# Windowed attention and a two-layer MLP on one core: another first load, another mask tile and another order of work for batch 0

## The chip, the core and the metric

The kernel runs on one core of a Trainium2 chip. The core has a matrix engine (TensorE, PE in the profile; its weight loads are listed as PEld), a vector engine (DVE), a scalar engine (ACT), GpSimd (POOL) and a queue engine (SP). POOL and SP issue the DMAs of this kernel. The metric is the device time of one execution in microseconds (us); lower is better. Three executions of the kernel before took 336.78, 336.99 and 338.26 us.

## The reference

Inputs are q, k and v of shape 8 batches x 8 heads x 576 positions x 64, and two weight matrices, 512 x 2048 and 2048 x 512, all in float32.

```python
scores = scale * np.matmul(q, k.transpose(0, 1, 3, 2))
rel = pos[:, None] - pos[None, :]
mask_plain = (rel >= 0) & (rel < window)                                # window 32
mask_dil = (rel >= 0) & (rel < window * dilation) & (rel % dilation == 0)  # dilation 4
masks = np.stack([mask_plain if h < H // 2 else mask_dil for h in range(H)], axis=0)
...                                   # softmax over the masked scores, attn @ v
x = attn_out.transpose(0, 2, 1, 3).reshape(B * S, H * D)                # 4608 x 512
h = x @ w_in
g = h * (1.0 / (1.0 + np.exp(-h)))
return (g @ w_out).astype(np.float32)
```

The first four heads look at the last 32 positions; the other four look at 32 positions that are 4 apart. Within one class of positions modulo 4 the second kind is the first kind again, on 144 positions.

## The kernel before, in words

**Two kinds of heads.** In the code z is the kind: z=0 the plain heads, z=1 the dilated ones, whose positions are sorted into four classes. Queries are taken 32 at a time against 64 keys. A score tile holds four such blocks in its 128 rows, and blocks of 64 columns side by side; one block of columns is called a slot.

**One batch of attention** goes through these helpers. `load_qk` and `load_v` issue the DMAs on POOL, which turn float32 into float16 on the way. `transpose` turns q and k on TensorE (16-bit transposes into PSUM) and copies them out on DVE and ACT. `scores` multiplies q and k (`score`, `score_class`, and `last_scores` for the 64 last positions), and adds mask and scale on DVE (L459, L468); L475 takes maxima. `exps` runs on ACT, either slot by slot with sums (L507), or in one instruction after `shift` has subtracted the maxima on DVE. `normal` divides on DVE (L516 to L523), `turn` and `turned` transpose the probabilities and copy them (L532, L540), `values` and `last_values` multiply with v (L565, L628), and `finish` casts the result into xT (L641). v lies in the tile vw; `shift_v` (`shift_class`, `shift_over`, `shift_plain`) copies parts of it to other rows, since blocks overlap by 32 keys.

**The MLP.** `layer1` makes, for each of 16 slices f of the hidden width, 128 x 576 values with eight matmuls (L654) and a silu on ACT. `layer2` makes 128 rows of output in 16 matmuls (L715) and stores them: a copy on DVE, a DMA on SP.

**Batch 0 is special.** Its q and k come in two parts of positions, 0 to 255 and 256 to 575 (`load_qk0`). The first part lies on 32 rows with 8 positions each, the second on 80 rows with 4 positions each (`URA`). `transpose0`, `masks0`, `scores0`, `maxima0`, `shift0`, `values0` and `finish0` work by parts. Here the mask is not added on DVE: `masks0` first writes it into PSUM with a matmul of the identity and the mask (`mask_b`), and the scores are added to it. The second part has its last slots in a PSUM tile of their own (`ss`), so that maxima and shifts there are two instructions each. Layer one of batch 0 is cut the same way (`layer1_part`, L674): two slices f and one part of the positions to a step, 16 steps. Layer two of batch 0 is `layer2_first` (L691), four steps by hidden slices, four row tiles in each.

**Order.** Every engine works through its instructions in the order in which the program emits them. The start is written out line by line at the end of the kernel. From layer one on, `plan_of(b)` names for each step what is emitted ahead of it: `at(step, function, ...)`. For batch 0 step s runs from -16 to -1 and 0 to 15 in pairs ahead of the 16 parts of layer one (part x gets steps 2x-16 and 2x-15), and from 16 to 31 ahead of groups of four matmuls of layer two. There also stands the work of batch 1: its transposes, scores, exps, values. Loads for later batches are planned the same way.

**Buffers.** PSUM has two large tiles (pool `big`: score tiles of batch 0, layer one, layer two) and four smaller ones (pool `ps`: transposes, scores of later batches, probabilities, values). A tile that is asked for waits until the one before it in the same buffer was read. `keep_busy` are matmuls whose result nobody reads.

**DMAs.** POOL issues all loads on one queue; eight semaphores go round, so that a load waits for the landing of the load eight before it.

## Time and profile before

| | |
|---|---|
| median of three runs | 336.99 us (336.78 to 338.26) |
| the profiled execution | 338.69 us, its span 336.9 us |
| PE busy | 317.1 us, 94% of the span, 5204 matmuls |
| ACT busy | 217.8 us, 65% |
| DVE busy | 180.5 us, 54% |
| POOL busy | 82.3 us, 24% |
| DMA | 32.16 MB moved, 44196 packets |
| shares of the chain that ended last | PE 85%, DVE 6%, ACT 4%, issue 3%, DMA 2% |
| layer one of batch 0 (L674) starts | 24.6 us |
| layer one of batch 1 (L654) starts | 74.1 us |

How to read it: the profile shows one execution. Its page gives the busy time of each engine, the span in 40 equal slices with a digit for each engine (9 is 90% or more), the DMA queues, the chain of work that ended last (followed from the last instruction back, at each step to what released it), and the costliest groups of instructions. "Issue" in the chain is time in which an engine waited for nothing that the profile shows. The timeline gives instructions with start and duration, in square brackets the idle time of the engine ahead of them and what ended it. The clock row (PEclk) is the TensorE clock that the throttle granted.

### The profile page before, as it was taken

The page shows a single profiled execution, that of the slowest core. Times are in us where ns is not written, and L with a number is a line of the kernel's source. Part 1 is how long each engine was busy: PE and PEld are TensorE (multiplying, and loading weights), DVE is VectorE, ACT ScalarE, POOL GpSimd, SP SyncE. Part 2 cuts the span into 40 slices and gives each one's busy share as a digit, 9 for nine tenths or more (in the row PEclk, how much of TensorE's full clock was granted, in tenths as well). Part 3 has the DMA queues.
Part 4 walks back from the last instruction along what each step waited for, and adds up shares of the span by engine and source line. Part 5 has one row for each costly group of instructions (what it writes and reads, how often), then busy time and mean ns, then how long its engine had stood idle before and what let it go on. Part 6 is the DMA issues. An engine that isn't in the chain of part 4 may idle for free.

```text
span 336.9 us, 11873 instructions
## 1 busy us (share of the span) xinstructions
PE 317.1 (94%) x5204; PEld 204.9 (61%) x5204; DVE 180.5 (54%) x377; ACT 217.8 (65%) x706; POOL 82.3 (24%) x139
## 2 busy tenths in 40 slices
PE   5778998699999999999999999999999999999995
PEld 2546753357745577557755578458755577467644
DVE  7676176843667755575556445675556533440011
ACT  1665667426699956996589556995699456916300
POOL 8436547540500443044301550042000000000000
PEclk9999997999999999999999999999999999999999
DMA  7999999992632499039802990059002100110021
GB/s 102 181 215 203 191 206 194 126 175 63 82 64 95 69 134 144 33 89 159 127 4 77 156 188 18 33 103 131 4 16 80 64 4 2 63 64 0 2 93 64
DMA packets 44196, 32.16 MB, mean 95 GB/s; under 512 B 21168, under 2 KB 38448, under 8 KB 44144
## 3 DMA queue, kind: packets, MB, share of 16 engines
q0 software_dynamic: 38480, 21.73, 46.7%
q1 hardware_dynamic: 5664, 9.67, 7.9%
q8 instruction: 40, 0.66, 0.8%
q14 instruction: 12, 0.10, 0.1%
HBM read 37.75 MB, written 9.44 MB: 140 GB/s over the span
## 4 chain that ended last, share of the span: by engine, by line
PE 85%; DVE 6%; ACT 4%; issue 3%; DMA 2%; POOL 0%; POOLq 0%
PE h L654 33%; PE o L715 31%; PE h L674 4%; PE t L270 3%; PE x L565 2%; PE pt L532 2%; PE o L691 2%; ACT pe L507 2%; DMA n<-in_q_dram 2%; PE s L338 2%; PE s L326 2%; DVE pn L523 1%; DVE nm L475 1%; DVE ms L459 1%; PE t L316 1%
## 5 line engine op out<-in xcount | busy, mean ns | idle before, releaser
L662 ACT ACTIVATE gT<-h 128x576 f16<-128x576 f32 x112 | 72.8, 650 | 68.0 <-PE h L654 67.5
L715 PE MATMUL o<-w_out,gT 128*128 128x512 f16 (+1 forms) x528 | 115.8, 373 | 0.5 <-DVE ob_last L724 0.5
L654 PE MATMUL h<-xT,w_in 128*128 128x288 f16 x896 | 115.4, 286 | 0.0
L654 PEld LDWEIGHTS <-w_in 128*128 128x128 f16 x896 | 85.7, 98 | 23.1 <-DVE ob L700 0.4
L507 ACT ACTIVATE pe<-ms,nm 128x64 f32<-128x64 f32 x246 | 81.6, 333 | 2.2 <-DVE nm L475 2.1
L715 PEld LDWEIGHTS <-gT 128*128 128x128 f16 x528 | 50.1, 98 | 53.6 <-issue 0.7
L700 DVE COPY ob<-o 128x512 f32<-128x512 f32 x35 | 24.1, 689 | 54.5 <-PE o L715 51.1
L507 ACT ACTIVATION_READ_ACCUMULATOR pe<-ms,nm 128x1 f32 x246 | 46.0, 187 | 0.0
L459 DVE SCALAR_TENSOR_TENSOR ms<-s,mask 128x512 f32<-128x512 f32 x28 | 19.2, 686 | 37.2 <-PE ss L326 21.3
L127 POOL DMA_DIRECT2D vw<-in_v_dram x16 | 10.0, 632 | 88.0 <-PE x L565 87.9
L523 DVE TENSOR_TENSOR pn<-pe,r 128x640 f16<-128x640 f32 (+2 forms) x32 | 25.3, 792 | 1.1
L641 DVE CAST xT<-x 128x512 f16<-128x512 f32 x26 | 16.8, 685 | 12.5 <-PE xs L628 12.5
L475 DVE TENSOR_REDUCE nm<-ms 128x10 f32<-128x640 f32 (+1 forms) x28 | 22.0, 786 | 1.0
L105 POOL DMA_DIRECT2D n<-in_k_dram x28 | 16.4, 596 | 15.3 <-PE t L270 11.5
L105 POOL DMA_DIRECT2D n<-in_q_dram x28 | 16.3, 598 | 15.1 <-DMA w_in<-in_moe_w_in_dram 9.2
L674 PE MATMUL h<-xT,w_in 128*128 128x320 f16 (+1 forms) x128 | 18.8, 305 | 0.8 <-DVE xT L633 0.7
L540 DVE COPY ptT<-pt 128x640 f16<-128x640 f16 (+1 forms) x27 | 11.7, 468 | 9.7 <-PE pt L532 9.5
L681 ACT ACTIVATE gT<-h 128x512 f16<-128x512 f32 (+1 forms) x16 | 10.4, 650 | 9.3 <-PE h L674 9.3
L691 PE MATMUL o<-w_out,gT 128*128 128x512 f16 x64 | 16.4, 407 | 0.0
L674 PEld LDWEIGHTS <-w_in 128*128 128x128 f16 x128 | 12.9, 104 | 5.6 <-issue 1.0
L532 PE MATMUL pt<-ident,pn 128*128 128x128 f16 x152 | 12.8, 227 | 3.7 <-DVE pn L523 2.0
L532 PEld LDWEIGHTS <-pn 128*128 128x128 f16 x152 | 10.4, 102 | 5.2 <-DVE pn L523 2.8
(102 smaller groups left out, 275.7 us busy)
## 6 DMA issues: line engine op xcount, KB each, us to landing
out_dram<-ob SPq DMA_DIRECT2D x35, 256.0 KB, 2.0
n<-in_k_dram POOLq DMA_DIRECT2D x28, 144.0 KB, 5.4
n<-in_q_dram POOLq DMA_DIRECT2D x28, 144.0 KB, 5.8
vw<-in_v_dram POOLq DMA_DIRECT2D x8, 288.0 KB, 5.7
vw<-in_v_dram POOLq DMA_DIRECT2D x16, 128.0 KB, 5.0
w_out<-in_moe_w_out_dram POOLq DMA_DIRECT2D x4, 512.0 KB, 10.1
vw<-vw POOLq DMA_DIRECT2D x12, 128.0 KB, 3.2
w_in<-in_moe_w_in_dram POOLq DMA_DIRECT2D x2, 512.0 KB, 11.0
```

Source lines behind the costliest of these rows:

```text
L105: nc.gpsimd.dma_start(out=qk[b, z, which][i * HF : i * HF + UPS[z]].rearrange("p h u d -> p h (u d)"), in_=src[b, h : h + 2].rearrange("h ...
L459: nc.vector.scalar_tensor_tensor(out=ms[:, 0:8].rearrange("p (n t) c -> p n (t c)", n=2), in0=s[hi].rearrange("p n t c -> p n (t c)"), sca ...
L475: nc.vector.tensor_reduce(out=nm[:, 0:w], in_=ms[:, 0:w], axis=AX.X, op=ALU.max, negate=True)
L507: nc.scalar.activation(pe[:, t, :], slot(t), AF.Exp, scale=1.0 if b else scale, bias=nm[:, t : t + 1], accum_out=l[:, t : t + 1],)
L523: nc.vector.tensor_tensor(pn[:, 0:w], a["pe", z, hi][:, 0:w], r[:, 0:w, None].broadcast_to([P, w, KB]), ALU.mult)
L532: nc.tensor.transpose(t[:, i, :], a["pn", z, hi][:, 2 * i : 2 * i + 2].rearrange("p t c -> p (t c)"), ident)
L654: nc.tensor.matmul(h[:, half, 0:HS], w_in16[:, c, f * P : f * P + P], xT[:, c, half * HS : half * HS + HS], start=(c == 0), stop=(c == MC ...
L662: nc.scalar.activation(gT[:, f, s0 : s0 + S].rearrange("p (a c) -> p a c", a=2), h[:, :, 0:HS], AF.Silu)
L674: nc.tensor.matmul(h[:, i, 0 : c1 - c0], w_in16[:, c, (f + i) * P : (f + i + 1) * P], xT[:, c, c0:c1], start=(c == 0), stop=(c == MC - 1),)
L691: nc.tensor.matmul(o, gT[:, f, t * P : (t + 1) * P], w_out16[:, f, :], start=(f == 0), stop=(f == NFF - 1),)
L700: nc.vector.tensor_copy(ob, o)
L715: nc.tensor.matmul(o[:, part, 0:m] if last else o[:, 0], gT[:, f, t * P : (t + 1) * P], w_out16[:, f, part * m : (part + 1) * m] if last e ...
```

## The change

- The first part of batch 0's q and k is loaded on 64 rows with 4 positions each, like the second part (`UR`), so `transpose0` has one form.
- At the start k is turned for both kinds of heads ahead of q. k and q of the dilated heads are copied by DVE, those of the plain heads by ACT. Then come both kinds' scores.
- `mask_b` has two of its four slots left and is made straight from `band`; the float32 `mask` of the later batches is made after q's copy, and `clear_v(1)` after the second maximum. The last slots of the second part lie in the same PSUM tile as the others, so that maxima and shifts are one instruction each. In this layout, slots of z=0 with odd blocks hold the other head of a pair (`hi ^ c % 2`), and `values0` reads them accordingly.
- w_in's last half is loaded by two DMAs.
- Layer one of batch 0 takes all slices of part 0, then all of part 1. Attention of part 1 is planned over the first eight.
- Batch 1's transposes and scores are planned earlier (both scores inside layer one), its exps of z=0 at step 16, its values at 25 and 29; the shifts of its v (`shift_v`) go from DVE to DMAs on SP.

```diff
-URA = (8, 4)
+UR = DIL
...
-    mask_b = cpool.tile([P, 2, 4, KB], BF16, name="mask_b")
+    mask_b = cpool.tile([P, 2, 2, KB], BF16, name="mask_b")
+    band_b = cpool.tile([P, KB], BF16, name="band_b")
...
-    load_w_in(2, 4)
+    load_w_in(2, 3)
+    load_w_in(3, 4)
...
+    def lay_mask(m):
+        n = 2 * m.shape[2]
+        nc.vector.tensor_copy(
+            m.rearrange("p a t c -> p (a t) c"), band[:, None, :].broadcast_to([P, n, KB])
+        )
+        nc.vector.memset(m[0:W, 0, 0, 0:W], NEG)
+        nc.vector.memset(m[:, 1, 0, 0:W], NEG)
+
+    lay_mask(mask_b)
     nc.vector.tensor_copy(ident_b, ident)
-    nc.vector.tensor_copy(mask_b, mask)
-    clear_v(1, nc.vector)
+    nc.vector.tensor_copy(band_b, band)
...
     def masks0(z, part):
-        sd = big.tile([P, 2, 512], F32, tag="big", name=f"s0_{z}_{part}")
...
+        n = width(0, z, part) // 2
+        s = big.tile([P, 2, 512], F32, tag="big", name=f"s0_{z}_{part}")
+        s = s[:, :, 0 : n * KB].rearrange("p h (t c) -> p h t c", c=KB)
         for h in (0, 1):
...
+            if part:
+                o, m = s[:, h], band_b[:, None, :].broadcast_to([P, n, KB])
+            else:
+                o = s[:, h].rearrange("p (n t) c -> p n (t c)", n=2)
+                m = mask_b[:, z].rearrange("p t c -> p (t c)")[:, None, :].broadcast_to([P, 2, 2 * KB])
+            nc.tensor.matmul(o, ident_b, m, start=True, stop=False)
+        att(0)["s", z, part] = s
...
     def maxima0(z, part):
         a = att(0)
+        w = width(0, z, part)
         nm = a["nm", z, part] = stat.tile([P, WM], F32, tag="nm", name=f"nm_0_{z}_{part}")
-        for i, m, s in pieces0(z, part):
-            nc.vector.tensor_reduce(
-                out=nm[:, i].rearrange("p (m t) -> p m t", m=m), in_=s, axis=AX.X, op=ALU.max, negate=True
-            )
+        nc.vector.tensor_reduce(
+            out=nm[:, 0:w].rearrange("p (h t) -> p h t", h=2), in_=a["s", z, part],
+            axis=AX.X, op=ALU.max, negate=True,
+        )
...
-            at(-14, shift_class, 0, nc.vector.tensor_copy, 1, 2)
+            at(-15, shift_class, 0, dve, 1, 2)
             at(-14, normal, 0, 0, 1)
-            at(-12, turn, 0, 1, 1)
-            at(-12, turned, 0, 1, 1, act)
-            at(-12, values0, 1, 1)
...
-            at(-10, turn, 0, 0, 1)
...
-            at(-8, values0, 0, 1)
...
-            transposes(at, 1, 1, 6)
-            at(10, scores, 1, 1)
+            at(-8, turn, 0, 1, 1)
+            at(-8, turned, 0, 1, 1, act)
+            at(-6, values0, 1, 1)
...
+            at(-4, turn, 0, 0, 1)
...
+            at(-2, values0, 0, 1)
...
+            transposes(at, 1, 1, 4)
+            at(7, scores, 1, 1)
             for hi in (0, 1):
-                at(10, shift, 1, 1, hi)
-            transposes(at, 1, 0, 14)
-            at(17, scores, 1, 0)
-            at(23, shift_v, 1, nc.vector.tensor_copy)
+                at(7, shift, 1, 1, hi)
+            transposes(at, 1, 0, 9)
+            at(13, scores, 1, 0)
+            at(14, shift_v, 1, nc.sync.dma_start)
...
             all_exps(1, 1)
-            for hi in (0, 1):
-                at(17, exps, 1, 0, hi)
-            later(at, 1, 1, (18, 19, 22, 24), both)
-            later(at, 1, 0, (20, 21, 23, 25), both)
+            all_exps(1, 0)
+            later(at, 1, 1, (18, 19, 23, 25), both)
+            later(at, 1, 0, (20, 23, 27, 29), both)
...
     load_qk(1)
...
+    keep_busy(big.tile([P, 2, 512], F32, tag="big", name="busy"), 4)
+    masks0(1, 0)
+    masks0(0, 0)
+    for which in (1, 0):
+        transpose0(0, 1, which, dve)
+        transpose0(0, 0, which, act)
+    lay_mask(mask)
+    scores0(1, 0)
+    scores0(0, 0)
+    maxima0(1, 0)
+    shift0(1, 0)
+    exps(0, 1, 0)
+    maxima0(0, 0)
+    scaled0(0, 0)
+    clear_v(1, nc.vector)
...
+    for which in (1, 0):
+        transpose0(1, 1, which, act)
     normal(0, 1, 0)
     exps(0, 0, 0)
     masks0(1, 1)
     scores0(1, 1)
     maxima0(1, 1)
     shift0(1, 1)
+    for which in (1, 0):
+        transpose0(1, 0, which, act)
     turn(0, 1, 0)
     turned(0, 1, 0, act)
-    transposes0(1, 0, (act, act))
-    exps(0, 1, 1)
+    normal(0, 0, 0)
     shift_class(0, dve, 0, 1)
-    normal(0, 0, 0)
+    shift_plain(0, dve, 0, 4)
     masks0(0, 1)
     scores0(0, 1)
-    values0(1, 0)
     turn(0, 0, 0)
     turned(0, 0, 0, act)
+    exps(0, 1, 1)
     maxima0(0, 1)
-    shift0(0, 1)
-    shift_plain(0, dve, 0, 4)
-    finish0(1, 0, (act, act))
-    exps(0, 0, 1)
+    values0(1, 0)
+    finish0(1, 0, both)
     warm = big.tile([P, 2, 512], F32, tag="big", name="h_0_0_0")
-    keep_busy(warm, 2)
+    keep_busy(warm, 1)
     values0(0, 0)
-    keep_busy(warm, 2)
-    finish0(0, 0, (dve, act))
+    finish0(0, 0, both)
+    shift0(0, 1)
+    exps(0, 0, 1)
+    keep_busy(warm, 2)
     load_qk(2)
...
-            units = [(0, 0), (0, 4), (1, 0), (1, 4), (0, 8), (0, 12), (1, 8), (1, 12)]
-            for x, (part, f) in enumerate([(p, f + i) for p, f in units for i in (0, 2)]):
+            for x in range(NFF):
                 plan(2 * x - NFF)
                 plan(2 * x + 1 - NFF)
-                layer1_part(f, part, None if x else warm)
+                layer1_part(2 * x % NFF, 2 * x // NFF, None if x else warm)
```

More of the change, by code (lines that the diff above doesn't have):

```diff
@@ L53 @@
     SA = NS // 2
[L54 to L55 removed]
+    PA = SA // UR
+    PB = (S - SA) // UR
     WM = 12
@@ L292, in transpose0 @@
         t0, n = ((0, PA), (SA, PB))[part]
-        ur = URA[part]
-        t = ps.tile([P, 2 * ur, n], F16, tag="ps", name=f"t{which}_0{part}_{z}")
+        t = ps.tile([P, 2 * UR, n], F16, tag="ps", name=f"t{which}_0{part}_{z}")
         if z:
-            t = t.rearrange("d (e m) p -> d e m p", m=8)
             for h in range(HH):
-                for u in range(0, ur, 2):
+                for u in range(0, UR, 2):
                     nc.tensor.transpose(
-                        t[:, u // DIL, 2 * h + u % DIL // 2, :],
+                        t[:, 2 * h + u // 2, :],
                         src[0:n, HP + h, u : u + 2, :].rearrange("p u d -> p (u d)"),
@@ L313, in transpose0 @@
         for i in (0, 1):
-            for u in range(ur):
+            for u in range(UR):
                 for hi in (0, 1):
@@ L353, with last_scores @@
     order = [[(c, hi) for c in range(4) for hi in (0, 1)], [(c, hi) for hi in (0, 1) for c in range(4)]]
-    def last_scores(b, z, ss):
+    def last_scores(b, z, last, first=True):
         for n in (0, 1):
@@ L833, in plan_of @@
         return plan
-    def transposes0(part, z, copies):
-        for which in (1, 0):
-            transpose0(part, z, which, copies[which])
     def keep_busy(tile, n):
```

120 lines of the change are left out of this document (39 added, 81 removed).

## The prediction

> **What bounds the kernel now.** I read the page's slices first, then the chain of work that ended last, then the timeline up to 75 us, at last the DMA issues. The slices (40 of 8.4 us):
>
> ```profile
> PE   5778998699999999999999999999999999999995
> ...
> PEclk9999997999999999999999999999999999999999
> ...
> GB/s 102 181 215 203 191 206 194 126 175 63 82 64 95 69 134 144 33 89 159 127 4 77 156 188 18 33 103 131 4 16 80 64 4 2 63 64 0 2 93 64
> ...
> q8 instruction: 40, 0.66, 0.8%
> ```
>
> TensorE is full from the ninth slice to the end, and nothing there changes but what is said below of code blocks. The loose time lies before 74 us: PE at 5 to 9 tenths, one slice with a lower clock, DMA near 200 GB/s up to 60 us. The chain names the pieces:
>
> ```profile
> 14.57 0.61 PE s L338 x20
> 15.23 0.72 issue
> ...
> 20.11 0.43 PE pt L532 x3
> 20.55 1.61 issue
> ...
> 24.78 3.43 PE h L674 x16
> 28.23 0.60 ACT gT L681
> 28.83 0.80 ACT ptT L540
> ...
> 50.95 1.55 issue
> ...
> 74.16 4.01 PE h L654 x32
> ```
>
> Layer one of batch 0 (L674) starts at 24.6 and of batch 1 (L654) at 74.1. Between them TensorE needs, from rows: layer one 7.0 us at the full rate (eight groups of 0.88) and 8.7 (eight of 1.09), turns and values of batch 0's second part 1.9, transposes and scores of batch 1 0.70 + 0.76 + 0.68 + 0.65, layer two 64 x 216 ns = 13.8, turns and values of batch 1 0.9 + 1.9: 37.0. It takes 49.5. The 12.5 us of slack are what this change can win or lose.
>
> **"Issue" in the chain is code.** The page's q8 moves 0.66 MB in 40 packets for 5204 matmuls and 5204 weight loads: one packet per 260 instructions. In the timeline there are 128 matmuls and 128 weight loads between the stop that ends at 15.96 and the one that ends at 22.15. The stops that end at 46.55 (0.44 us) and 52.50 are 256 apart too. So a block of 256 PE instructions takes 6.2 and 5.95 us to come while the DMA queues are full, and PE stops if it is faster; blocks of small matmuls are.
>
> ```profile
> 50.45 0.50 PE L326 MATMUL s<-kT,qT 64*32 64x64 f16 x42 [0.66 <-DVE qT L274]
> ...
> 52.50 0.35 PE L326 MATMUL s<-kT,qT 64*32 64x64 f16 x22 [1.55 <-issue]
> ...
> 52.89 5.96 PE L691 MATMUL o<-w_out,gT 128*128 128x512 f16 x20
> ```
>
> The last line is the clock: seven of these 20 matmuls follow each other at 425 ns, the rest at 216. L674's first 16 take 3.43 us (213 ns each); later groups of eight take 0.88.
>
> **The change, step by step** (in the profiled execution: 338.7 us, span 336.9; the median of the runs shown is 336.99, 1.7 below the profiled one).
>
> 1. *First loads.* q lands at 2.02 + 5.7 = 7.7, k at 5.5. The loads of 80 rows already have the new pieces (256 numbers): they land 2.2 us apart for 640 pieces, so 512 would take 1.8 against 2.2 now: 0.4 to 0.8 us earlier. Against that, DMA moves 169 GB/s at 5 to 7.75 us (old pieces) and 140 at 7.75 to 10 (new ones): 512 KB then take 0.6 us longer. I take 7.7, nothing gained; ends -0.8 and +0.6.
>
> 2. *Transposes and masks.* 96 transposes of the first part become 48, 8 or 16 to a tile; at 67 ns (80x80 row) and about 30 ns that is 0.5 us each for q. k's copies now lie on DVE and ACT while q is on its way. On DVE the big mask (0.74 + 0.2) moves from before the loads to between q's copy and the first maximum, and clear_v(1) (1.7) from before the loads to after the second maximum. The path: q 7.7, turned 8.3, qC on DVE 0.69 to 9.0, mask to 9.9, maximum and shift 0.69 each to 11.3 (now 11.1), z0's maximum 12.0, scaling 12.3, clear 14.1, then sums, reciprocals and pn (0.68 + 0.4 + 0.69) to 16.1 (now 15.3). One reduction and one shift over 12 tiles (0.95 each) replace 0.69 + 0.42 and 0.68 + 0.41: 18.1. pn of z0 0.3 + 0.2 + 0.69: 19.3; v's shifts 0.48 + 0.42 + 0.35: 20.6; maximum 0.82; two xT casts 0.42 each: 22.3. ACT beside it: q part 1 lands at 12.2, two copies, eight exps 2.6, two copies, ptT: 18.5; the second ptT waits for pn (19.3): 20.5, then exps of (1,1) to 21.4. So L674 starts at 22.5, now 24.6: **2.1 us earlier**; ends 0.5 and 3.
>
> 3. *Code in the head.* The chain above has now two stops, 0.72 and 1.61. With 48 transposes fewer and other masks, the block that now starts inside the scores of (1,1) starts at the scores of (0,1), which wait for qT until 17.9 anyway, and the next one in layer one's third group, 25.8, against 17.9 + 6.2 = 24.1. Both stops go; that is in the 22.5.
>
> 4. *Layer one part by part.* Now the second part's xT is needed in the fifth group, and PE waits 0.9 for ACT's ptT (28.7 to 29.7) and 0.9 before 33.56. Afterwards eight groups of part 0 cover it: ptT, casts and values have a whole group (0.88) before they are needed; a wait of 0.5 is left. Sum: two groups at half clock 3.4, six 5.3 and 0.4 for the third, partly slow, turns and values 1.9, waits 0.5: part 1 starts at 34.0. Now the same work would stand at 33.56 + 4 x 0.88 = 37.1. **Lead 3.1.** The last quarter of w_in is needed at 31; in two pieces it lands by about 28 (now 27.0, +0.6 as in 1): hidden.
>
> 5. *Batch 1 in layer one.* Eight groups 8.7, transposes 0.70 + 0.76, scores 0.68 + 0.65. Now z=0's scores wait 0.7 for qT and 1.55 for code, inside layer two. Afterwards: q's second turn comes 1.1 us after scores that hold three of the four PSUM buffers (freed by L459 and L468, 2.6 us on): 1.0. Then some 256 instructions (half the scores, three groups, 72 transposes) are through in 4 us instead of 6: a stop of 1.8. Copies 0.5. Layer two starts at 48.8, as now (48.8), but with z=0's scores done. On DVE, q and k of z=0 wait behind two shifts (1.5); that runs beside the stop.
>
> 6. *Layer two.* 13.8 + 0.9 + 1.9. exps start after the last silu (50.3): table 1.28, 2 x 0.7, 18 x 0.33 = 5.9, ptT 0.7, so 59.6, where PE arrives at 58.5: 1.1. A last wait for the copies out 0.4. Layer one of batch 1 would start at 66.9, with no half clock. With the stops of step 5 (2.8 us in 4) the clock may fall as it does now after 2.2 us in 3: 0 to 1.7, I take 0.8: 67.7, now 74.1. **Lead 6.4.** The four v shifts that leave DVE (0.68 + 0.42 + 0.78 + 0.87, in the chain) go to SP; they wait there for v, landed by 42, have until 56, and stores stand behind them only from 65.
>
> 7. *Later batches.* Same order, but the program has 106 PE instructions fewer, so blocks of code begin 106 places later in the work. Now blocks last 4.4 us or more and stop PE for 0.80 (95.5) and 0.28 (168). Read off the timeline, shifted ones last 3.4 (from 89.4) and 3.8 to 4.2 (123.7, 146, 159, 183, 198.6, 234, 257, 273). That is nine. The first meets 90 us, where eight q,k loads are in flight: 2.4 lost. The others have 95 to 188 GB/s or nothing beside them: 0 to 1 each, 1 in all. Less the 1.1 that go: **2.2 lost**; ends 0 and 6.
>
> Sum: -6.4 + 2.2 = -4.2: 336.99 - 4.2 = 332.8. Without the unknowns -8 (329); with them all bad about 0.
>
> [...] Rows: 256 instructions never came in under 5.9 us while loads ran, and PE stood 0.7 to 1.6 us. [...]
>
> [...] Rows: half rate after two stops of 2.2 us together. [...]
>
> **Rivals.** (a) Code never stops PE anew: the 1.8 of step 5 and the 2.2 of step 7 fall away, 332.8 - 4.0 = 328.8. For it: blocks of 4.7 to 4.9 us pass unhurt after 100 us. Against: four stops before 53 us. 0.12. (b) Code eats the lead: the nine shifted blocks of step 7 meet loads. A block then costs 5.9 less its own length, 2.5 for the first and about 1.9 for each other. With the first and three others the lead of 6.4 is gone (2.5 + 5.7 - 1.1 = 7.1); with five others the time is 336.99 - 6.4 + 10.9 = 341.5, slower; with two 335.8, no change. Against: at 118 to 135 us (134 and 144 GB/s) present blocks of 4.9 us do not stop. No change 0.12, slower 0.06. (c) The clock stays at half past 26 us, since values and turns break up layer one; each group of part 0 then loses 0.82. With the remaining six and four of part 1 (1.09 each) 9.3 are lost: 342. It decides from 6 us of half clock gained on, at about 36. Against: it rises now 5 us after layer one starts, with a 0.9 us hole in it. 0.04.
>
> **Numbers.** Forecast 332.8, chance 0.66, own range 330 to 335; (a) 0.12; no change 0.12; slower 0.10. 0.5% (1.7 us) is what a measurement can tell: faster 0.78, same 0.12, slower 0.10. Range 329.0 to 336.6: it leaves out (b)'s and (c)'s upper end and half of (a).
>
> **What would show it.** Step 2, 3: no "issue" over 0.3 between 12 and 24 us, L664 (layer one by parts) at 22.5. Step 4: part 1's 128x320 at 34, without a wait above 0.5. Step 5: "issue" of about 1.8 near 43. Step 6: L644 at 67 to 68, no vw copy of batch 1 on DVE. Step 7: an "issue" near 83 to 90. The prediction is wrong if L644 starts later than 72, or if stops after 70 us sum to more than 5.

## The result and the profile after

In the comparison the changed kernel took 334.86 us (median of 15 executions, 333.15 to 337.02) and the kernel before 338.09 (15 executions, 336.26 to 341.06): ratio 0.9906, 95% interval 0.9879 to 0.9934, so 2.2 to 4.1 us less. The forecast was 332.8 in a range of 329.0 to 336.6. The profiled executions differ by more than the medians, 336.9 against 332.6 us of span: 4.3 less. Executions of one kernel lie up to 5 us apart here, and part of the reason is found below; times are therefore compared as medians with their intervals, and profiles are used for where and why.

From the page of the changed kernel, the slices (40 of 8.3 us) of TensorE's work and its granted clock, and the queue of code:

```profile
PE   5779889998999999999999979999999999999995
...
PEclk9999979999999999999999999999999999999999
...
q8 instruction: 40, 0.66, 0.8%
```

PE is nearly full from the seventh slice on. The lower clock is still there, one slice earlier than before (the sixth, 42 to 50 us), and the 24th slice has a new hole. The chain that ended last (start, duration, what):

```profile
14.04 0.46 issue
14.49 12.79 DMA n<-in_k_dram
...
40.77 2.25 issue
43.02 3.24 PE h L664 x13
...
67.68 3.94 PE h L644 x32
...
75.90 0.86 issue
...
196.24 1.88 issue
198.12 0.27 PE ss L336 x11
198.38 4.03 PE h L644 x32
```

Of TensorE's two stops in the head, 0.72 and 1.61, none is left: the 0.46 at 14.04 is POOL's, between the scores and the load that it issues at 14.49, while TensorE goes from the scores into turns at 13.94 without a pause. A stop of 2.25 stands in layer one, and two stand in the later batches. Layer one by parts (L664) starts at 21.57, before 24.57; layer one of batch 1 (L644) at 67.52, before 74.08. From there to the end of the span it is 265.1 us, before 262.8. So 6.56 us are won before batch 1 and 2.26 lost behind it.

The timeline of TensorE in layer one of batch 0, second part (start, duration, line and operation, count; in brackets the idle time ahead and what ended it), and the clock in windows of 2 us (the last three figures: granted clock, DMA share, GB/s):

```profile
39.59 0.67 PE L274 MATMUL t<-ident,n 64*64 64x64 f16 x36 [0.80 <-DMA vw<-in_v_dram]
40.19 0.58 PE L664 MATMUL h<-xT,w_in 128*128 128x320 f16 x3
43.02 3.24 PE L664 MATMUL h<-xT,w_in 128*128 128x320 f16 x13 [2.25 <-issue]
```

```profile
44.00:46.00 2.00, 2.00 (x9) 0.98 (x7) 0.00 (x0) 0.70 (x1) 0.56 (x1) 0.50 1.18 251
46.00:48.00 2.00, 2.00 (x81) 1.46 (x81) 0.99 (x2) 0.70 (x1) 0.20 (x1) 0.77 1.19 215
```

The stop comes after three matmuls of a group, at no buffer and no operand: PE waits for its next block of code (its packet in the queue of code starts at 40.70 and ends at 41.64, 1.38 before PE goes on), and when it goes on, thirteen matmuls take 3.24 us where 13 at full rate (136 ns) would take 1.8. The clock was at one half.

### The profile page after: what moved, and what is told of

Read it like the earlier page. It is cut to its first block, busy times and chain, and to the rows that moved or that the text cites. A ratio compares the mean times of both kernels' runs of the same rounds, so it can differ in the third digit from the quotient of the medians.

```text
span 332.6 us, 11772 instructions
## 1 busy us (share of the span) xinstructions
PE 313.6 (94%) x5151; PEld 202.5 (61%) x5151; DVE 179.0 (54%) x375; ACT 216.3 (65%) x703; POOL 83.5 (25%) x140
## 4 chain that ended last, share of the span: by engine, by line
PE 79%; DMA 8%; ACT 5%; issue 3%; POOL 2%; DVE 2%; POOLq 0%
PE h L644 34%; PE o L705 31%; DMA n<-in_k_dram 4%; ACT pe L496 4%; PE t L274 3%; PE x L554 3%; DMA vw<-in_v_dram 2%; DMA n<-in_q_dram 2%; PE pt L521 2%; PE o L681 2%; PE s L336 1%; PE s L324 1%; PE h L664 1%; POOL n L118 1%; POOL w_out L186 0%
## 5 line engine op out<-in xcount | busy, mean ns | idle before, releaser
L644 PE MATMUL h<-xT,w_in 128*128 128x288 f16 x896 | 115.4, 286 | 0.0
L644 PEld LDWEIGHTS <-w_in 128*128 128x128 f16 x896 | 85.7, 98 | 23.0 <-DVE ob L690 0.3
L448 DVE SCALAR_TENSOR_TENSOR ms<-s,mask 128x512 f32<-128x512 f32 x28 | 19.2, 687 | 38.5 <-PE ss L324 18.9
L512 DVE TENSOR_TENSOR pn<-pe,r 128x640 f16<-128x640 f32 (+2 forms) x32 | 25.3, 792 | 1.1
L664 PE MATMUL h<-xT,w_in 128*128 128x256 f16 (+1 forms) x128 | 19.6, 307 | 2.9 <-issue 2.2
L664 PEld LDWEIGHTS <-w_in 128*128 128x128 f16 x128 | 12.7, 104 | 7.8 <-issue 3.9
L681 PE MATMUL o<-w_out,gT 128*128 128x512 f16 x64 | 14.8, 379 | 0.0
L274 PEld LDWEIGHTS <-n 64*64 64x64 f16 (+1 forms) x840 | 10.1, 101 | 5.6 <-issue 3.8
```

Of the source, the lines that this page charges most:

```text
L274: nc.tensor.transpose(dst, w, ident[r, r])
L448: nc.vector.scalar_tensor_tensor(out=ms[:, 0:8].rearrange("p (n t) c -> p n (t c)", n=2), in0=s[hi].rearrange("p n t c -> p n (t c)"), sca ...
L512: nc.vector.tensor_tensor(pn[:, 0:w], a["pe", z, hi][:, 0:w], r[:, 0:w, None].broadcast_to([P, w, KB]), ALU.mult)
L644: nc.tensor.matmul(h[:, half, 0:HS], w_in16[:, c, f * P : f * P + P], xT[:, c, half * HS : half * HS + HS], start=(c == 0), stop=(c == MC ...
L664: nc.tensor.matmul(h[:, i, 0 : c1 - c0], w_in16[:, c, (f + i) * P : (f + i + 1) * P], xT[:, c, c0:c1], start=(c == 0), stop=(c == MC - 1),)
L681: nc.tensor.matmul(o, gT[:, f, t * P : (t + 1) * P], w_out16[:, f, :], start=(f == 0), stop=(f == NFF - 1),)
```

## The experiments

Each kernel was profiled once and timed against the kernel before. The first table puts all in one place; "layer one" is the start of batch 0's, "batch 1" the start of batch 1's layer one, "rest" the time from there to the end of the span, all from the one profile, and the ratio is that of the medians. Kernels with the same head agree in the first column to half a microsecond (before, e1, e2, e12) or to 0.01 (changed, e3, e6 to e9).

| kernel | layer one | batch 1 | rest | median us | ratio to before, 95% |
|---|---|---|---|---|---|
| before | 24.57 | 74.08 | 262.8 | 338.09 | |
| changed | 21.57 | 67.52 | 265.1 | 334.86 | 0.9906 (0.9879 to 0.9934) |
| e1 order alone | 24.33 | 72.11 | 262.7 | 336.47 | 0.996 (0.994 to 0.998) |
| e2 batch 1's plan alone | 24.06 | 72.15 | 263.4 | 337.03 | 0.9975 (0.9952 to 0.9998) |
| e3 head alone | 21.57 | 69.91 | 265.5 | 335.11 | 0.9906 (0.9878 to 0.9934) |
| e6 head and order | 21.57 | 68.45 | 263.3 | 334.22 | 0.9895 (0.9864 to 0.9927) |
| e4 changed, 106 more | 21.93 | 68.81 | 264.5 | 334.95 | 0.992 (0.9891 to 0.9949) |
| e5 changed, load on 32 rows | 22.77 | 68.92 | 262.9 | 333.84 | 0.9872 (0.9828 to 0.9917) |
| e7 changed, loads held | 21.57 | 66.26 | 263.9 | 331.61 | 0.9791 (0.9748 to 0.9835) |
| e8 changed, 160 more | 21.58 | 68.02 | 262.6 | 331.86 | 0.9807 (0.9768 to 0.9845) |
| e9 e7 and e8 | 21.58 | 68.19 | 261.8 | 330.98 | 0.9769 (0.9736 to 0.9801) |
| e10 e7, memsets later | 19.89 | 66.88 | 263.4 | 331.99 | 0.9829 (0.9789 to 0.9869) |
| e11 all three | 20.46 | 63.91 | 261.8 | 327.94 | 0.9717 (0.9674 to 0.9761) |
| e12 before, loads held | 24.05 | 72.08 | 262.5 | 336.82 | 0.9966 (0.9939 to 0.9994) |

### The parts of the change, alone and together

e1 is the kernel before with the order of layer one and batch 0's plan for it:

```diff
-            at(-12, turn, 0, 1, 1)
+            at(-8, turn, 0, 1, 1)
...
-            units = [(0, 0), (0, 4), (1, 0), (1, 4), (0, 8), (0, 12), (1, 8), (1, 12)]
-            for x, (part, f) in enumerate([(p, f + i) for p, f in units for i in (0, 2)]):
+            for x in range(NFF):
...
-                layer1_part(f, part, None if x else warm)
+                layer1_part(2 * x % NFF, 2 * x // NFF, None if x else warm)
```

> The kernel before with one part of the change: layer one of batch 0 part by part, and attention of batch 0's second part planned over the first eight groups. First loads, masks, head and batch 1's plan stay as before, and so do the 5204 matmuls, so blocks of code begin at the same counts of instructions. Theory (step 4 of the prediction): the two waits of 0.9 us for ptT and the one for xT go, part 1 stands 3 us ahead at equal work; layer one of batch 1 (L654) starts at 71 to 72 instead of 74.1, since the stop for code in the scores of z=0 grows by about 1 when PE arrives sooner; time 2 to 3 us below before (ratio 0.991 to 0.994). Rival: the second part's chain or the next stop for code takes the gain, L654 starts at 73.5 or later, ratio 0.998 or more.

e2 is the kernel before with batch 1's plan:

```diff
-            transposes(at, 1, 1, 6)
-            at(10, scores, 1, 1)
+            transposes(at, 1, 1, 4)
+            at(7, scores, 1, 1)
...
-            transposes(at, 1, 0, 14)
-            at(17, scores, 1, 0)
-            at(23, shift_v, 1, nc.vector.tensor_copy)
+            transposes(at, 1, 0, 9)
+            at(13, scores, 1, 0)
+            at(14, shift_v, 1, nc.sync.dma_start)
...
-            later(at, 1, 1, (18, 19, 22, 24), both)
-            later(at, 1, 0, (20, 21, 23, 25), both)
+            all_exps(1, 0)
+            later(at, 1, 1, (18, 19, 23, 25), both)
+            later(at, 1, 0, (20, 23, 27, 29), both)
```

> The kernel before with only batch 1's plan changed: its transposes and scores inside layer one, exps of z=0 at step 16, values later, and the shifts of its v on SP instead of DVE. 5204 matmuls as before. Theory (steps 5 and 6 of the prediction, 6.4 less the 3.1 of step 4): L654 starts about 3.3 us earlier, at 70.8, with no 0.7 wait for qT and no 1.55 stop inside layer two, but a stop of 1 to 2 us inside layer one; time 2.5 to 3.5 us below before (ratio 0.990 to 0.993). Rival: what goes from layer two comes back in layer one whole, as waits for PSUM and for code; L654 at 73.5 or later, ratio 0.998 or more.

e3 is the changed kernel with both of these undone, so that the head alone is left:

> The changed kernel with layer one's order and both plans (batch 0's and batch 1's) as before: what is left of the change is the head, with the loads on 64 rows, k turned ahead, the mask tiles, the one PSUM tile, and 106 PE instructions fewer than before. Theory: layer one (L664) starts at 21.6 as in the changed kernel, 3.0 ahead of before; some of it is lost again in layer one's waits for ptT and xT, since the work of ACT and DVE behind them is as long as it was; L644 starts at 72 to 73, and with blocks of code that begin 106 places later the time is 0 to 2 us below before (ratio 0.994 to 1.000). Rival (the head's gain goes through whole, as a sum of steps takes it): L644 at 71.1 or earlier, and what the steps of order and batch 1's plan bring are then 3.5 us together.

and e6 has head and order, that is the changed kernel with batch 1's plan undone:

> The changed kernel with batch 1's plan as before: head and order are left of the change, 5151 matmuls. In the traces layer one of batch 1 starts at 69.9 with the head alone, 72.1 with the order alone, 72.1 with batch 1's plan alone and 67.5 with all. If order and head add (4.2 + 2.0), L644 starts at 67.9 here, and batch 1's plan is worth 0.4 in company against 1.9 alone, since its scores meet a stop for code inside layer one. If the order is what brings nothing in company, L644 starts at 69.5 to 70. Stop at 196 as in the changed kernel (1.9) in both cases.

Measured at the start of batch 1's layer one: order 2.0 us, plan 1.9, head 4.2 earlier than before. One after the other it is head 4.2, with the order 5.6, with the plan 6.6: in company the order brings 1.5 and the plan 0.9. Each of these figures is from one execution. In the profiles of before, the changed kernel, e1 and e6 the clock, once it has risen, falls to one half again for 3.41 us before batch 1, which is worth up to 1.7; in those of e2 and e3 it does not. So up to 1.7 of the plan's 1.9 and of the head's 4.2 can be that, and this column doesn't settle differences of 1 to 2 us. The theory of e1 was missed at that place by a hair (72.11 for "71 to 72") and in the time (0.994 to 0.998, expected 0.991 to 0.994). In e3 the rival's number came there, 69.91 for 71.1 or earlier, though with that half clock it might not have. e6 lies between its two cases (68.45 for 67.9 or 69.5 to 70), and its stop at 196 is 1.40 and not 1.9. In e2 neither number of the theory nor the rival's came: 72.15 lies between. The timeline of e2 shows both mechanisms at work:

```profile
45.01 0.77 PE L270 MATMUL t<-ident,n 64*64 64x64 f16 x49 [2.07 <-issue]
45.71 2.35 PE L674 MATMUL h<-xT,w_in 128*128 128x320 f16 x16
47.99 0.67 PE L326 MATMUL s<-kT,qT 64*32 64x64 f16 x62
51.40 0.20 PE L326 MATMUL s<-kT,qT 64*32 64x64 f16 x2 [2.75 <-issue]
51.59 2.35 PE L674 MATMUL h<-xT,w_in 128*128 128x320 f16 x16
```

Layer two of batch 0 with what is put between lasts 18.4 us here and 25.3 before, 6.9 less, as the plan means; but layer one ends 5.0 later (its last matmul at 53.64 against 48.63), and 4.8 of that are two stops for code. Transposes and scores, which are many small instructions, were brought together in less time than their code took to come here.

In the whole time, head alone and the full change have the same ratio. The intervals are about 1 us wide to each side, so up to some 2 us for order and plan together are not excluded; none are shown. In the profile of e3 the same stop as in the changed kernel, in the later batches, is followed by half clock (chain):

```profile
197.50 1.94 issue
199.44 0.27 PE ss L336 x11
199.71 5.70 PE h L644 x32
```

5.70 us for 32 matmuls that take 4.03 in the changed kernel behind its stop of 1.88. So one such stop costs 1.9 in one execution and 3.6 in another. That is the size of the scatter between executions. The mean granted clock of each execution points the same way: 3.41 us at one half lower it by 0.005. Of the changed kernel's fifteen, the only one at 1.00 is the fastest (333.15), eight at 0.994 or 0.995 took 334.06 to 335.88, and the five from 0.985 to 0.990 took 335.02 to 337.02. (One at 0.969 took 334.48; half clock in the head counts too where the records reach back that far, as in e2's profile, where it lasts from 9.4 to 26.5 us.)

### Does the load on 64 rows matter?

e5 is the changed kernel with `URA = (8, 4)` again for the loads and the turns of the first part:

```diff
-UR = DIL
+URA = (8, 4)
...
-            copy(dst[:, :, :, i0 : i0 + n].rearrange("d h r p -> d (h r) p"), t)
+            copy(
+                dst[:, :, :, i0 : i0 + n * e].rearrange("d h r (p e) -> d (h r) p e", e=e),
+                t.rearrange("d e m p -> d m p e"),
+            )
```

> The changed kernel with the first part of q and k on 32 rows with 8 positions each again (and its 96 transposes for 48, copies with two interleaved runs), all else as changed; 96 PE instructions more, so blocks of code begin nearly where they do in the kernel before. Steps 1 and 2 of the prediction took nothing from the load (q at 7.7 either way) and 0.5 us from the transposes. If that is so, q lands at 6.8 to 7.0 here too and layer one (L664 of the changed kernel) starts at 22.1. Rival: the load on 64 rows is itself faster by the 0.5 to 0.9 us by which q landed earlier, and the copies on DVE by 0.27 each (0.42 against 0.69): q at 7.5 to 7.7, layer one at 23.0 to 23.5. Time: the changed kernel's plus 0 to 2 us by either.

q lands at 7.23, in the changed kernel's profile at 6.80, but that decides nothing: in e7, whose head is that of the changed kernel, it lands at 7.21, and layer one starts at 21.57 as well. TensorE of the changed kernel, at the head:

```profile
5.69 1.03 PE L380 MATMUL s<-mask_b,ident_b 128*128 128x256 bf16 x4 [0.39 <-DVE ident_b L240]
6.66 0.60 PE L301 MATMUL t<-ident,n 64*128 64x64 f16 x8
7.19 0.64 PE L314 MATMUL t<-ident,n 64*64 64x64 f16 x16
7.76 0.61 PE L301 MATMUL t<-ident,n 64*128 64x64 f16 x8
```

Masks wait for DVE's `ident_b`, then come k's turns, then at 7.76 q's, without a pause. In e5 q's turns start at 7.99; the turns of the plain heads take 1.04 instead of 0.64 each time, so the scores start at 9.49 instead of 8.88 and the first maximum at 10.16 instead of 9.55. Layer one starts 1.2 later, 0.36 of it a stop for code. Neither expectation was met: 22.77 lies between 22.1 and 23.0, and q's landing plays no part in it. The copies on DVE are what was not foreseen (e5, then the changed kernel):

```profile
7.13 0.69 DVE L312 COPY kC<-t 128x512 f16<-128x512 f16 x1 [1.56 <-PE t L304]
```

```profile
7.29 0.42 DVE L308 COPY kC<-t 128x512 f16<-128x512 f16 x1 [1.38 <-PE t L301]
```

In the whole time e5, expected 0 to 2 us slower, is not (0.9872, interval to 0.9917, which overlaps the changed kernel's): the 96 instructions it has more put its blocks of code nearly where they lie before, and "rest" is 262.9 where the changed kernel has 265.1.

### Do the stops belong to blocks of code?

e4 and e8 put 106 and 160 PE instructions at the start, in place of a part of `keep_busy`; nobody reads what they compute.

```diff
-    keep_busy(big.tile([P, 2, 512], F32, tag="big", name="busy"), 4)
+    busy = big.tile([P, 2, 512], F32, tag="big", name="busy")
+    keep_busy(busy, 2)
+    for x in range(82):
+        r, c = x % 2 * HF, x // 2 % 2 * HF
+        nc.tensor.matmul(
+            busy[c : c + HF, x % 2, 0:QB], ident[r : r + HF, r : r + HF],
+            ident[r : r + HF, r : r + QB], start=True, stop=True,
+        )
```

(e4: three of `keep_busy` and 54 small ones.)

> The changed kernel with 106 PE instructions more at its start: three of the four matmuls that keep TensorE busy, then 54 of 64x64 by 64x32, whose results nobody reads either. Blocks of code begin at the same work as in the kernel before. Theory (step 7): the stops of 0.86 us at 75.9 and 1.88 at 196 belong to blocks and go; what comes instead are before's own, 0.8 in layer two's scores near 90 and 0.3 near 162, so 1.1 to 1.7 less in all after 67 us: span 331 to 331.5 if layer one of batch 1 still starts at 67.5; the 2.25 at 40.8 moves too, by an unknown amount (-2 to +1). Rival: the stops belong to the instructions that stand there (their waits or buffers); then they stay where they are, and the span is 332.6.

> The changed kernel with 160 PE instructions more at its start (two of the four matmuls that keep TensorE busy, then 82 small ones). Blocks of code begin 160 instructions earlier in the work than in the changed kernel, 54 earlier than in the kernel before. If stops belong to blocks, those at 40.8, 75.9 and 196 go or move: the boundary of 40.8 now falls at the scores of z=1 near 37, where three groups of layer one before it give the fetch 4 to 5 us: a stop of 1 to 1.5 there; no stop above 1 in the later batches, since each boundary falls into matmuls of layer one or two. Span 330 to 331.5. If stops went with the instructions they would stay, 332.6.

Chain of e4:

```profile
39.40 2.27 issue
46.98 1.09 issue
90.20 1.29 issue
163.17 1.20 issue
```

Chain of e8:

```profile
43.80 1.64 issue
...
89.31 0.65 issue
```

The stops at 75.9 and 196 are gone in both, though the instructions that stood there are the same with the same waits. For 196 this holds over all profiles: a stop of 1.33 to 1.94 begins between 194 and 198 in the five kernels with 5151 matmuls (changed, e3, e6, e7, e10) and in none of the others. The one at 75.9 stands in no other profile, those five included, so its absence here shows nothing; its packet of code alone took 3.0 us where others take about 1. In e4 those of the kernel before come back, at its places (z=0's scores of layer two, and a transpose near 163). They are larger, 1.29 and 1.20 for 0.80 and 0.28, and layer one got a second stop, so e4 gains nothing (span 333.3, expected 331 to 331.5). In e8 "rest" is 2.5 us shorter than in the changed kernel, and the time 3 us (0.9807, the interval lies below the changed kernel's). The place of a stop in e8 was expected at the scores of z=1; it came in the group after them (1.35 at 37.85) and once more in z=0's scores (1.64 at 43.80). The stops belong to blocks of 256 instructions: in the changed kernel 512 matmuls, each with its weight load, lie between the ends of the stops at 40.77 and 75.90, four blocks of 128, and 2175 from there to the end of the one at 196, 17 blocks with one record short. Which way to lay the blocks is best has to be tried.

### What makes a block late?

e7 holds the second half of w_out and batch 2's q and k back, e12 does the same to the kernel before, e9 puts e7 and e8 together:

```diff
-    load_w_out(2)
-    load_w_out(3)
...
-    load_qk(2)
...
+            at(8, nc.vector.memset, w_out16[:, 2 * DIL, 0:1], 0.0)
+            at(8, load_w_out, 2)
+            at(8, load_w_out, 3)
+            at(8, load_qk, 2)
```

> The changed kernel, but the second half of w_out and batch 2's q and k are loaded later: a memset of one column on DVE at step 8 holds POOL's queue until about 39 us. So 2.2 MB are not in flight at 37 to 40 us, where the block of code is asked for that PE waits 2.25 us for at 40.8. Theory (a block comes late because loads are in the queues): the stop shrinks to 1 or less, layer one of batch 1 starts 1.2 to 3 us earlier (66.3 to 64.5, the larger figure if the half clock of 43 to 46 us goes as well), time 1 to 2.5 us below the changed kernel's. Rival (a block takes its 3.5 us whatever is in the queues, or the loads held back meet the next block): the stop stays at 2 or more, or one of that size follows before 55; time within 0.7 of the changed kernel's.

> Both earlier edits together: the loads held back until step 8, and 160 PE instructions more at the start. If the loads set how late a block comes and the places of the blocks set where that hurts, the gains add in part: layer one of batch 1 at 66 to 66.5 (66.3 with the hold alone, 68.0 with the 160 alone), and from there to the end no stop above 0.7, as with the 160 alone (262.6 us from L644 to the end of the span, against 265.1 in the changed kernel): span 328.6 to 329.5, time 330.3 to 331.2. Rival: the places move so that new stops of over 1 us come in layer one; L644 at 67.5 or later, time 331.6 or more.

> The kernel before with its loads of w_out's second half and of batch 2's q and k held back in the same way, by a memset at step 8, which DVE reaches at about 42.6 us here. It asks whether the hold is worth 3 us to either order of work. Over the profiles so far a block is asked for when PE enters the one ahead of it, and its packet starts after 2.9 us (median) where over 180 GB/s move and 1.6 at 80 to 140. Theory: the packets of before that start at 44.3 and 49.9 come some 1 us sooner, so the stop of 1.55 that ends at 52.5 shrinks to 0.5 or less, the half clock behind it (1.5 us) goes, layer one of batch 1 starts at 71.5 to 73 instead of 74.1, time 1 to 2.5 us below before. Rival (the hold pays only in the changed order): the stop stays over 1.2, or the loads held back meet the blocks of 50 to 60 us, L654 at 73.8 or later, time within 0.7 of before.

e7, timeline:

```profile
38.32 0.39 PE L336 MATMUL s<-kC,qC 64*32 64x64 f16 x28 [1.50 <-issue]
...
43.10 1.94 PE L664 MATMUL h<-xT,w_in 128*128 128x320 f16 x13 [0.68 <-issue]
```

e9, timeline:

```profile
41.24 1.12 PE L664 MATMUL h<-xT,w_in 128*128 128x320 f16 x4 [3.17 <-issue]
```

e12, timeline:

```profile
50.05 0.28 PE L326 MATMUL s<-kT,qT 64*32 64x64 f16 x22 [0.43 <-issue]
```

By the medians the hold gains 3.2 us in the changed kernel (0.9791, the interval below the changed kernel's), 1.1 in the kernel before, and nothing that can be told apart when the 160 instructions are there already (e9 0.9769, e8 0.9807, overlapping). The stop of 2.25 went down to 0.68 as the theory has it, but one of 1.50 came a block earlier; what went for good in that profile is the half clock. In e12 the stop fell from 1.55 to 0.43 and the half clock behind it went, as expected, with L654 at 72.08; the time is 1.1 lower, at the low end of what was expected. In e9 the stop at 38 us is the longest of all and L644 is at 68.19, as the rival has it, though the time, 330.98, lies in the theory's range. Part of e7's gain can be the clock: three of its four executions have a mean of 1.000, and one of the changed kernel's fifteen; that is up to 1.7 of the 3.2. e8's four, all at 0.993 to 0.995, gain their 3.0 without it. So a single stop doesn't decide. All fourteen profiles together say more. For each block I took from the trace the time from PE's first instruction in the block before it to the start of its packet in the queue of code, and what the other queues moved in between:

```
moved meanwhile   blocks   quartiles of the time, us
under 80 GB/s        345   -0.8   0.5   0.9
80 to 140             24    1.0   1.6   2.0
140 to 180            70    1.6   2.5   3.3
over 180             120    1.8   2.9   3.6
```

(Below zero: the packet started ahead of PE's arrival.) When a block is asked for stands in no record; that PE's entry into the block ahead sets it, as e7 and e12 take it, is an estimate from these times. The packet then took about 1.0 us, and where PE stood waiting it went on 1.3 to 1.6 us after the packet's end. Over 180 GB/s a block thus needed 2.9 + 1.0 + 1.4 = 5.3 us in the middle and up to about 7 (e10: 4.7 + 0.9 + 1.4), under 80 GB/s about 3 (0.5 + 1.0 + 1.4). That code comes late where loads are in flight is shown by the groups, which compare different places of the program. That the loads are the cause is supported by the two stops that shrank when loads were held back (e7, e12), and not by e9. Which load delays which packet is open: the packet that starts 2.0 us after PE enters a block at 28.28 in e8 starts 4.1 after it in e9, at the same time of the same work, with the same loads issued up to there.

### Does DVE set the start of layer one?

e10 is e7 with `clear_v(1)` and the loads behind it at the end of the head:

```diff
-    clear_v(1, nc.vector)
-    load_w_out(0)
-    load_w_out(1)
-    load_v(1)
...
     keep_busy(warm, 2)
+    clear_v(1, nc.vector)
+    load_w_out(0)
+    load_w_out(1)
+    load_v(1)
```

> The kernel with the loads held back, and clear_v(1) with the first half of w_out and batch 1's v emitted at the end of the head, behind the last shift of the first scores. In the trace of the changed kernel the four memsets of clear_v(1) stand on DVE from 11.7 to 13.7 in the chain that ends at layer one; q's landing (6.8) does not: the turns of q begin at 7.8, after k's. If DVE is the path, sums start at 11.8, probabilities of z=1 are out at 13.5 and layer one (L664) starts 0.8 to 1.5 us earlier, at 20.1 to 20.8; ACT (exps, two copies, to 16.7) is late next. Of that lead little reaches batch 1 if code sets the pace to 45 us: L644 between 65.2 and 66.3, time 330.5 to 331.7. Rival: ACT or a stop for code ends where DVE ended, L664 at 21.2 or later.

> All three edits: loads held back, 160 PE instructions more at the start, clear_v(1) at the end of the head. If they add: L664 at 20.1 to 20.8, L644 at 65 to 66, no stop over 0.7 after it, span 327.6 to 329, time 329.4 to 330.7. If code sets the pace to 45 us, L664's lead is eaten by the next stop, L644 at 66 to 67 and the time is that of the kernel with two edits.

DVE in the changed kernel is busy from 8.40 to the end of the head, and four memsets stand in it ahead of the sums:

```profile
11.60 0.17 DVE L412 TENSOR_SCALAR nms<-nm 128x8 f32<-128x8 f32 x1
...
11.95 0.48 DVE L195 MEMSET vw<- 32x512 uint32 x1
...
13.22 0.48 DVE L197 MEMSET vw<- 32x512 uint32 x1 [0.16 <-issue]
...
13.74 0.69 DVE L505 TENSOR_REDUCE l<-pe 128x8 f32<-128x512 f32 x1
```

Without them layer one starts at 19.89 in e10 and 20.46 in e11, 1.7 and 1.1 earlier, in e10 a little more than expected: DVE was the path, not q. (The edit moves three loads too, and q's second part is turned at 10.85 in e10 instead of 11.68. That it was DVE is read from its row, where one instruction follows another, and not from a run that moves the memsets alone.) In e10 the lead went into the next block of code, as feared (timeline of e10):

```profile
19.89 2.96 PE L664 MATMUL h<-xT,w_in 128*128 128x256 f16 x16
...
42.24 3.42 PE L664 MATMUL h<-xT,w_in 128*128 128x320 f16 x13 [2.87 <-issue]
```

L644 is at 66.88, 0.6 later than in e7 and later than the expected 65.2 to 66.3, with half clock again; the time, 331.99, is no gain over e7's 331.61. In e11 it was kept (timeline of e11):

```profile
20.46 2.79 PE L664 MATMUL h<-xT,w_in 128*128 128x256 f16 x16
...
38.30 0.72 PE L664 MATMUL h<-xT,w_in 128*128 128x320 f16 x4 [1.57 <-issue]
...
63.91 4.09 PE L644 MATMUL h<-xT,w_in 128*128 128x288 f16 x32
```

One stop of 1.57, no half clock, L644 earlier than either expectation, span 325.7, median 327.94: 0.9717 of the kernel before (0.9674 to 0.9761). Its median is the lowest of all, 6.9 us below the changed kernel's; the intervals of e7 and e9 overlap with its own. Why e11 had a stop of 1.57 where e9 had 3.17 can't be read from the edits. Two of its six executions took 331.2 and 331.4, at a mean clock of 0.995 and 0.994; the four at 0.999 and 1.000 took 326.5 to 328.3. In e9 two at 0.998 and 1.000 took 328.3 and 329.1, and four at 0.990 to 0.995 took 330.8 to 331.8. So a part of e11's lead over e9 is that fewer of its executions fell to half clock, and with so few of them that can be chance.

## Why the prediction was right, step by step

The time came out 2.1 us above the forecast, inside the range, on the side that was given the highest chance. 1.1 of the 2.1 is the kernel before itself, whose repeated median is 338.09 and not 336.99; the change brought 3.2 in the medians and 4.3 between the two profiles, for a forecast of 4.2. The steps, against the profiles:

1. *First loads.* Taken as 7.7; q landed at 6.80, just beyond the lower end (7.21 and 7.23 in e7 and e5). But the step failed in another way: the landing was not on the path (e5, e7).
2. *Transposes and masks.* Predicted 2.1 us earlier, measured 3.0, at the upper end. The chain of steps was right: turned at 8.3 (8.40), clear to 14.1 (13.7), first probabilities 16.1 (15.6), casts. Mis-sized were the copy on DVE, 0.69 for 0.42, and the room between steps, and the reason of the first term: masks and k's turns on PE, not q's landing, lead to 8.3. What the step did not see as a gain to be had is that the clear could leave the path: 1.1 to 1.7 (e10, e11).
3. *Code in the head.* Both stops went, as predicted: the "issue" of 0.46 at 14.04 is POOL's and not a stop for code.
4. *Part by part.* Part 1 started at 32.1, not 34.0. 0.9 of it is step 2. The other 1.0 is the clock: two groups were taken at half rate, 16 matmuls of 213 ns, and in the changed kernel seven of them start 213 ns apart and the rest 109 (16 of 16 before). The third group's wait was another one than thought, 0.67 for the silu of the first, which comes behind the last shift on DVE, the exps and a table load of 1.28 on ACT. The wait of 0.5 at the ends became 0.17. (In the kernel before, the wait ahead of 33.56 is 0.73 by its row, not 0.9.)
5. *Batch 1 in layer one.* The right mechanism with the right place (40.8 for "near 43", with part 1 1.9 us ahead): PSUM 0.80 for 1.0, code 2.25 for 1.8. (The row of the 0.80 names a DMA; but L448, which frees a buffer of the scores, ends on DVE at 39.44 and TensorE goes on at 39.59, so either fits.) The stage took 17.0 us and not 14.8, since the half clock of step 6 came here. So all of the further lead of step 4 was gone at layer two: 49.15, predicted 48.8. That it comes so near is two errors that cancel, 1.9 us more lead and 2.2 us more stage.
6. *Layer two.* L644 at 67.5, predicted 67.7. The 0.8 put down for the clock, an estimate halfway between nothing and 1.7, is shown by no run: half clock cost 1.5 in this profile (13 matmuls in 3.24 for 1.77, in layer one already) and nothing in e7 and e11; as a mean of two outcomes it was fair, for one execution it can't be right.
7. *Later batches.* The sum is right by luck, 2.26 for 2.2 (its own terms, 2.4 + 1 - 1.1, give 2.3), since the places are wrong. The stops make 1.66 of it, 0.86 + 1.88 for 0.80 + 0.28; the rest was not traced. No stop came near 90; they came at 75.9 and 196, of which only the size was covered by the bounds. That the one at 196 belongs to a block, as the step said, is shown; its list of the nine blocks and the load beside each was not good enough to say which would stop.

Rival (a), code that never stops PE anew, is out: three new stops stand in the chain, 5.0 us together. Code came sooner where the queues were quiet: its packets started 0.5 us after PE entered the block ahead (median of 345 blocks under 80 GB/s), and 2.9 us after it over 180 GB/s (120 blocks). Rival (b) had the right mechanism with too many stops: two, 2.7 us together, of which the one at 196 may be the block listed at 198.6 and the other is in no list. It decided nothing here, but its range is real, since one stop can carry 1.7 us of half clock with it. Rival (c) did not come up: the matmuls go at the full rate from 23 us on, but for the 3.41 us of half clock from 43.5 on.

## What to carry to other kernels

Count instructions, not only their time: where loads filled the queues here (over 180 GB/s), every 256 TensorE instructions needed about 5.3 us for their code, and work of many small matmuls that is drawn together to fill a hole can open another one (e2: 2.07 and 2.75 us). A stop cost up to 1.7 us more than its length where it left TensorE idle for 1.9 us or more of one of the stretches of 3.41 us that the clock's changes mark here (next section). A change of the number of instructions moved the later stops (e4, e8), so it changes places that the diff does not touch; compare stages in the trace, and try a few shifts before judging a change of less than 1%. A head start is worth only what the next stop leaves of it: the same removal of four memsets brought 1.7 us at layer one and nothing in the median in one kernel (e10 against e7), and 1.1 at layer one and 3.0 in the median in another (e11 against e9), in whose profile the stop behind it was short.

## What the runs showed that was not expected

- *Stops of the same length were followed by half clock or not; in these profiles it went by how they fell into stretches of 3.41 us.* Half rate followed stops of 1.55 (before, with a wait of 0.66 just ahead), 1.64 (e8), 1.92 (e5), 1.94 (e3), 2.25 (changed), 2.27 (e4), 2.87 (e10) and 3.17 (e9); it did not follow 1.57 (e11), 1.88 (changed, at 196), nor 2.07 and 2.75 in e2. Each time it cost about 1.5 to 1.7 us. In the clock's records each spell of half rate between the head and the end of the span lasts 3.41 us, and the changes lie whole multiples of 3.41 apart (changed kernel: full from 23.01 for 20.48, half for 3.41, full for 286.72). Windows cut at these places, first of the changed kernel (the second figure is PE's busy time, the third from the end the granted clock):

```profile
40.07:43.49 3.42, 1.17 (x31) 0.65 (x18) 3.22 (x5) 0.64 (x1) 1.28 (x3) 1.00 1.25 232
43.49:46.90 3.41, 3.41 (x83) 1.95 (x81) 0.00 (x0) 1.31 (x2) 0.56 (x1) 0.50 1.22 244
```

Of e8:

```profile
42.95:46.37 3.42, 1.50 (x77) 1.06 (x77) 0.82 (x2) 0.70 (x1) 0.15 (x1) 1.00 1.21 244
46.37:49.78 3.41, 3.41 (x15) 1.91 (x13) 2.52 (x5) 0.70 (x1) 0.56 (x1) 0.50 1.19 229
```

Of e2:

```profile
46.98:50.39 3.41, 1.67 (x70) 1.09 (x68) 0.77 (x2) 1.41 (x2) 1.33 (x3) 1.00 1.21 213
50.39:53.81 3.42, 2.41 (x27) 1.75 (x28) 2.14 (x4) 0.70 (x1) 2.86 (x6) 1.00 1.17 203
```

Of e11:

```profile
35.92:39.33 3.41, 1.84 (x65) 1.05 (x51) 3.27 (x7) 0.34 (x2) 0.00 (x0) 1.00 1.84 169
```

The stop of 2.75 in e2 is longer than that of 1.64 in e8, but it is shared by two windows. Over all profiles that have records of the clock (13; e12's has none), from 22 to 320 us, ten windows had PE busy for at most 1.50 us, and after each of them the next one is at half rate; 1086 had 1.67 us or more, and after none of them it is. Ahead of 22 us this does not hold: in e2 a window with 2.4 us of work (6.0 to 9.4) was followed by half rate. The edges lie at other times from profile to profile (52.49 in before, 43.49 in the changed kernel, 46.37 in e8), and the windows ahead of half rate were not idle there: PE was busy in them for 1.21, 1.17 and 1.50 us. The row of granted clock doesn't show all of it: at 22 us it reads 1.00 in the changed kernel, where the matmuls start 213 ns apart. The records begin at 23.01 there, just where the spacing falls to 109.
- *Copies of equal shape on DVE differ by 0.27 us.* 128 x 512 numbers of 16 bits from PSUM took 0.42 where each run is written in order and 0.69 where two runs are interleaved (L308 against L312 of e5).
- *A memset was worth more than a faster load.* One column written by DVE, to hold a queue back, brought 3.2 us in the median, of which up to 1.7 can be the clock; q landing 0.4 us earlier or later brought nothing.
